# Talking-heads attention ahead of two feed-forward layers on one core: the mixed matrix and v kept in fp32 for their product, and the steps laid anew

## The chip, the cores and the metric

The kernel runs on one core of one Trainium2 chip. The metric is the device time of one execution in microseconds, the median over several runs. One further execution is recorded by the hardware profiler; every row below is from it.

## What is computed

```python
# q, k, v: (4, 12, 448, 64); w_pre, w_post: (12, 12)
scores = np.matmul(q, k.transpose(0, 1, 3, 2)) / 8
scores = np.einsum('bhij,hg->bgij', scores, w_pre)      # mix the heads
scores = scores - np.max(scores, axis=-1, keepdims=True)
attn = np.exp(scores)
attn = attn / (np.sum(attn, axis=-1, keepdims=True) + 1e-09)
attn = np.einsum('bhij,hg->bgij', attn, w_post)         # mix the heads again
x = np.matmul(attn, v)                                  # -> (1792, 768)
h = x @ w_in;  x = (h * np.cos(h)) @ w_out              # 768 -> 2048 -> 768
g = x @ w_gate                                          # 768 -> 1536
out = (g / (1 + np.exp(-g)) * (x @ w_val)) @ w_out2     # 1536 -> 768
```

All inputs and the output are fp32.

## The kernel before

**Attention.** Each of the 4 batches is cut along the queries into 4 chunks, and a chunk into 12, 12, 11 or 10 blocks (`CH`) of 10 queries by 12 heads. So there are 45 blocks in a batch and 180 in all. A block passes through these functions, one after another:

- `premix` (line 220): TensorE multiplies the block's scores, 120 rows by 448 keys, by a block matrix of w_pre. Both are fp32; each such matmul stands in the trace as two matmul records.
- `rowmax` (225, VectorE), `expo` (233, ScalarE), `den` (240) and `rec` (244, VectorE): the softmax.
- `norm_hi` (249, GpSimd) and `norm_lo` (256, VectorE): the normalized block as an fp16 value and an fp16 rest.
- `post` (269 to 271): 12 fp16 matmuls by w_post, 3 for each quarter of the keys. The result lies transposed in PSUM, 112 keys by 480.
- `at_hi` (282, ScalarE) and `at_lo` (290, VectorE): that result, copied out as fp16 value and fp16 rest.

Once for each chunk and pair of heads `m` (six of them) come two more products:

- `qk` (195): scores of the next chunk, 6 matmuls, 3 for each head of the pair; the two heads use different rows of TensorE. `spread` (211, 213) copies each head's scores to SBUF and sends them by a DMA on SP's queue into `x`, laid out for `premix`. `qk` uses the two PSUM banks `ps_s`.
- `pv` (302): the mixed matrix times v. v is split by `split_v` (176, 179, 182) into fp16 value and rest, so there are 12 products for each head: 4 quarters of the keys by 3 terms. The two heads use different columns of TensorE and lie in turn in the program. Three `m` share one of the two banks `ps_v`. `pv_out` (319, 320) takes three `m` out of PSUM.

v is loaded twice. The first time (`vm`) it is only read for its largest value (`max_v`, 148), from which `scale_v` makes a power of two, by way of a small TensorE matmul (`pow2_b`, 83). The second time (`vr`) it is scaled and split.

The order is written out by hand. `plan` holds for each step `i` which functions run; block `i` does `premix` at step `i` and each later function a fixed lag behind. `QK_STEPS` and `PV_STEPS` say at which steps of a chunk the six `qk` and `pv` stand. Inside a step, `order` sets the order of the functions, and so the order of the instructions on each engine. `dma_k`, `dma_q` and `dma_v` stand in the plan in the same way; all of these DMAs are issued on SP's queue.

**Feed-forward.** During the last chunk `early_plan` begins with the first layer (`l1_part`, 732 to 734; `hidden`, 749 to 762). After the attention `FeedForward.steps` runs the rest: weights are loaded, scaled and split (567 to 606), and `l2` (777 to 783) adds to the result. The change leaves this code as it is.

Of the kernel before, what the change touches and what calls it, by code (L numbers as in the profile page):

```python
# [20 lines left out]
DM = H * D  # L21
# [19 lines left out]
def attention(ctx, tc, qT, kT, vN, mix, xs, ff):  # L41
# [39 lines left out]
    def pow2_b(diag, n, name):  # L81
        ps = ps_v.tile([128, 512], F32, tag="pv", name=f"psp_{name}")
        nc.tensor.matmul(ps[:, :n], ones[:n, :], diag[:n, :n], start=True, stop=True)
        return ps
# [13 lines left out]

    ff.ps_sum = lambda name: ps_v.tile([128, 512], F32, tag="pv", name=name)
    ktiles, qtiles, vtiles, vscale = {}, {}, {}, {}  # L100
# [36 lines left out]

    def dma_v(b, jc, why):
        r = p_vr.tile([112, DM], F32, tag="vr", name=f"v{why}_{b}_{jc}")
        nc.sync.dma_start(r, vN[b, :, jc])  # L140
        raws["v", why, b, jc] = r

    vmx = {}

    def max_v(b, jc):
        if jc == 0:
            vmx[b] = p_small.tile([112, 4], F32, tag="vmx", bufs=2, name=f"vmx_{b}")
        nc.vector.tensor_reduce(
            out=vmx[b][:, jc:jc + 1], in_=raws.pop(("v", "m", b, jc)), axis=AX.X, op=ALU.max,
            apply_absolute_value=True,  # L150
        )
# [3 lines left out]
    def scale_v(b, part):  # L155
        if part == 1:
            scales[b] = pow2_b(scales[b], 112, f"v{b}")
            return
        if part == 2:
            p = pow2_c(scales[b], 112, f"v{b}")  # L160
            nc.vector.tensor_scalar(
                ff.unit[0][:, b:b + 1], p[:, 0:1], pw[:, 0:1], 2.0 ** -9, op0=ALU.mult, op1=ALU.mult
            )
            vscale[b] = p
            return
        m1 = p_small.tile([112, 1], F32, tag="vmx1", bufs=2, name=f"vmx1_{b}")
        nc.vector.tensor_reduce(out=m1, in_=vmx[b], axis=AX.X, op=ALU.max)
        scales[b] = pow2_a(m1, 112, f"v{b}")

    def split_v(b, jc, part):  # L170

        r = raws["v", "r", b, jc]
        rv = r.rearrange("p (m e d) -> p m e d", e=2, d=D)
        by = vscale[b][:112, 1:2]
        if part == 0:
            nc.scalar.activation(r, r, AF.Copy, scale=by)
        elif part == 1:
            t = vtiles[b, jc] = p_v.tile([112, 6, 2, 2, D], F16, tag="v", name=f"v_{b}_{jc}")
            nc.vector.tensor_copy(t[:, :, :, 0], rv)
        else:  # L180
            t, m = vtiles[b, jc], slice(3 * part - 6, 3 * part - 3)
            nc.gpsimd.tensor_tensor(t[:, m, :, 1], rv[:, m], t[:, m, :, 0], op=ALU.subtract)

    X, SP, SMALL, PM, E, EHL, PA, AT, PV = ({} for _ in range(9))

    def qk(b, c, m, places=((ps_s, "s"),)):

        n = 10 * CH[c]
        for e in range(2):
            pool, tag = places[(2 * m + e) % len(places)]  # L190
            SP[b, c, 2 * m + e] = pool.tile([128, 512], F32, tag=tag, name=f"pss_{b}_{c}_{2 * m + e}")
        for i, (zq, zk) in enumerate(((0, 0), (1, 0), (0, 1))):
# [80 lines left out]

    def at_hi(b, c, k):
        n = CH[c]
        if k == 0:
            AT[b, c] = tuple(
                p_at.tile([112, n, 4 * H, 10], F16, tag=f"at{z}", padded_shape=[112, 12, 4 * H, 10],
                          name=f"at{z}_{b}_{c}")
                for z in range(2)  # L280
            )
        nc.scalar.activation(
            AT[b, c][0][:, k].rearrange("p g i -> p (g i)"), PA[b, c, k][:112, :480], AF.Copy,
            scale=2.0 ** -4,
        )

    def at_lo(b, c, k):
        src = PA.pop((b, c, k))[:112, :480]
        th, tl = (t[:, k].rearrange("p g i -> p (g i)") for t in AT[b, c])
        nc.vector.scalar_tensor_tensor(tl, src, 2.0 ** -4, th, op0=ALU.mult, op1=ALU.subtract)  # L290

    def pv(b, c, m):


        n = 10 * CH[c]
        if m % 3 == 0:
            PV[b, c, m // 3] = ps_v.tile([128, 4, 128], F32, tag="pv", name=f"psv_{b}_{c}_{m}")
        ps = PV[b, c, m // 3]
        prods = [(jc, zv, za) for jc in range(4) for zv, za in ((0, 0), (0, 1), (1, 0))]
        for i, (jc, zv, za) in enumerate(prods):  # L300
            for e in range(2):
                nc.tensor.matmul(  # L302
                    ps[64 * e:64 * e + 64, m % 3, :n].rearrange("p (k i) -> p k i", i=10),
                    vtiles[b, jc][:, m, e, zv], AT[b, c][za][:, :, jc * H + 2 * m + e],
                    start=(i == 0), stop=(i == len(prods) - 1),
                )

    def pv_out(b, c, g3):
# [10 lines left out]
        nc.scalar.activation(hi, ps[:, :, :r], AF.Copy, scale=2.0 ** -5)  # L319
        nc.vector.scalar_tensor_tensor(lo, ps[:, :, :r], 2.0 ** -5, hi, op0=ALU.mult, op1=ALU.subtract)  # L320
        if not direct:
# [13 lines left out]
    for i, blk in enumerate(blocks):  # L335
        for fn, lag in ((premix, 0), (rowmax, 1), (expo, 1), (den, 2), (rec, 3), (norm_hi, 3),
                        (norm_lo, 4), (post, 6), (at_hi, 7), (at_lo, 7)):
            at(i + lag, fn, *blk)
    for ci, (b, c) in enumerate(chunks):
        n, s0 = CH[c], first[b, c]  # L340
        if ci + 1 < len(chunks):
            nb, ncn = chunks[ci + 1]
            for m in range(6):
                i = s0 + QK_STEPS[n][m]
                at(i, qk, nb, ncn, m)
                for e in range(2):
                    at(i + 1, spread, nb, ncn, 2 * m + e)
            if ci:
                at(s0 - 7, dma_q, nb, ncn)
                for e in range(2):  # L350
                    at(s0 - 2 + e, hi_q, nb, ncn, e)
                    at(s0 - 1 + e, lo_q, nb, ncn, e)
        if c == 2 and b + 1 < B:
            for m in range(6):
                i = s0 + 1 + 14 * m // 6
                at(i - 1, dma_k, b + 1, m)
                at(i + 2, hi_k, b + 1, m)
                at(i + 3, lo_k, b + 1, m)
        if c == 0:
            if b == 0:  # L360
                for part in range(3):
                    at(4 + part, scale_v, 0, part)
            if b + 1 < B:
                for part in range(3):
                    at(first[b, 3] + 7 + part, scale_v, b + 1, part)
            for jc in range(4):
                if b == 0:
# [7 lines left out]
                if b + 1 < B:  # L375
# [10 lines left out]
    for i, fn, *a in ff.early_plan(first[B - 1, 3]):  # L386
        at(i, fn, *a)

    order = (
        "rec", "pv_out", "pv", "post", "at_hi", "l1_part", "rowmax", "dma_v", "at_lo", "w_sum",  # L390
        "w_sum_all", "w_unit", "w_bits", "hidden", "den", "max_v", "scale_v", "hi_k", "dma_q",
        "lo_q", "spread", "split_v", "dma_k", "w_dma", "x_load", "load_next", "new_scale", "hi_q",
        "w_max", "w_shift", "w_split", "expo", "norm_hi", "premix", "qk", "lo_k", "norm_lo",
    )


    with tc.manual_schedule():
# [580 lines left out]
```

## Time and profile before

| | |
|---|---|
| median of 3 runs | 1462.12 us (1461.84 to 1464.26) |
| the profiled execution: its time, its span | 1462.24 us, 1460.4 us |
| span, PE busy | 1408.3 us, 96% |
| span, DVE / ACT / POOL busy | 73% / 44% / 34% |
| the first block's `premix`, the last chunk's first `premix` | 22.1 us, 435.0 us |
| matmuls of the feed-forward alone from | about 493 us |

PE is TensorE, PEld its weight loads, DVE VectorE, ACT ScalarE, POOL GpSimd, SP the queue that issues most DMAs. Matmuls are pipelined: a matmul's recorded time is longer than its share of the stream. So the time that a group of matmuls takes is read from its first start to the first start of the next group.

### The profile page before, as it was taken

What the parts mean: (1) busy time and instruction counts of PE and PEld (TensorE: products, weight loads), DVE (VectorE), ACT (ScalarE), POOL (GpSimd) and SP (SyncE); (2) the same over time, 40 slices, a digit from 0 to 9 for tenths busy, and PEclk for the clock granted to TensorE, in tenths of its full rate; (3) what the DMA queues carried; (4) which work ended last, traced back from release to release, by engine and by line L of the source; (5) the groups of instructions that cost most, each with busy time, mean ns of one, the idle gap of its engine ahead of it and who ended that gap; (6) DMA issues with size and microseconds to landing.
All of it is one profiled execution on the core that took longest, in us unless ns stands there. A gap on an engine that the chain in (4) does not pass through costs nothing.

```text
span 1460.4 us, 27063 instructions
## 1 busy us (share of the span) xinstructions
PE 1408.3 (96%) x10330; PEld 940.7 (64%) x10330; DVE 1068.1 (73%) x2310; ACT 646.3 (44%) x1374; POOL 494.4 (34%) x522
## 2 busy tenths in 40 slices
PE   6999999999999899999999999989999999999999
PEld 2556666656665566767676766656666666666666
DVE  5888989888988667878888878786355656565523
ACT  3777877877865353333333332444422223222210
POOL 2553553553532233323333332332223223222210
PEclk9999999999999999999999999999999999999999
DMA  6555555555546112121212221021112212211013
GB/s 203 147 155 152 154 157 157 149 156 149 156 140 226 44 55 77 54 66 54 77 54 66 65 65 44 22 65 55 55 44 66 66 44 69 62 55 33 1 38 114
DMA packets 102264, 131.77 MB, mean 90 GB/s; under 512 B 29848, under 2 KB 88696, under 8 KB 102136
## 3 DMA queue, kind: packets, MB, share of 16 engines
q1 hardware_dynamic: 101296, 128.77, 29.8%
q8 instruction: 81, 1.33, 0.4%
q10 hardware_dynamic: 840, 1.29, 0.3%
q14 instruction: 47, 0.39, 0.1%
HBM read 80.95 MB, written 10.37 MB: 63 GB/s over the span
## 4 chain that ended last, share of the span: by engine, by line
PE 76%; DVE 15%; ACT 4%; DMA 3%; issue 2%; SPq 0%; POOL 0%; ACTq 0%; DVEq 0%; POOLq 0%
PE ph L732 10%; PE ph L734 10%; PE ph L733 10%; PE psm L220 9%; PE py L777 7%; PE py L778 7%; PE py L779 7%; PE pss L195 5%; PE psv L302 4%; PE psa L269 3%; PE psa L270 2%; PE psa L271 2%; DVE acc L783 2%; DVE r L750 2%; DVE r L753 2%
## 5 line engine op out<-in xcount | busy, mean ns | idle before, releaser
L732 PE MATMUL ph<-x,h_i 128*128 128x448 f16 x960 | 339.4, 354 | 0.0
L733 PE MATMUL ph<-x,h_i 128*128 128x448 f16 x960 | 338.9, 353 | 0.0
L734 PE MATMUL ph<-x,l_i 128*128 128x448 f16 x960 | 338.9, 353 | 0.0
L762 POOL TENSOR_TENSOR gl<-r,gh 128x448 fp32r<-128x448 f32 x112 | 131.6, 1175 | 411.4 <-ACT gh L761 406.1
L777 PE MATMUL py<-gh,h_o 128*128 128x448 f32 x672 | 257.8, 384 | 11.5 <-DVE acc L783 6.2
L778 PE MATMUL py<-gl,h_o 128*128 128x448 f32 x672 | 245.5, 365 | 0.0
L779 PE MATMUL py<-gh,l_o 128*128 128x448 f32 x672 | 245.2, 365 | 0.1
L783 DVE TENSOR_TENSOR acc<-py,acc 128x448 f32<-128x448 f32 x288 | 174.4, 619 | 64.2 <-PE py L779 60.3
L220 PE MATMUL psm<-x,wpre_sb 120*120 120x448 f32 x360 | 181.1, 586 | 17.8 <-DMA x<-s 7.1
L249 POOL TENSOR_SCALAR eh<-e,sm 120x448 f16<-120x448 f32 x180 | 115.0, 639 | 183.8 <-DVE sm L244 113.9
L732 PEld LDWEIGHTS <-h_i 128*128 128x128 f16 x960 | 93.9, 98 | 92.4 <-issue 10.6
L777 PEld LDWEIGHTS py<-gh,h_o 128*128 128x128 f32 x672 | 127.3, 189 | 37.1 <-DVE acc L783 16.9
L734 PEld LDWEIGHTS <-l_i 128*128 128x128 f16 x960 | 94.0, 98 | 87.9 <-issue 0.4
L733 PEld LDWEIGHTS <-h_i 128*128 128x128 f16 x960 | 94.2, 98 | 82.0 <-issue 0.2
L225 DVE TENSOR_REDUCE sm<-psm 120x1 f32<-120x448 f32 x180 | 110.6, 615 | 41.7 <-PE psm L220 40.2
L233 ACT ACTIVATE e<-psm,sm 120x448 f32<-120x448 f32 x180 | 115.7, 643 | 56.9 <-DVE sm L225 55.1
L606 POOL TENSOR_TENSOR l_i<-f_i,h_i 128x384 f16<-128x384 f32 x80 | 81.3, 1016 | 174.9 <-ACT h_i L605 174.7
L760 DVE SCALAR_TENSOR_TENSOR r<-ph,by_i,r 128x448 f32<-128x448 f32 x48 | 32.8, 684 | 146.5 <-PE ph L734 115.8
L269 PE MATMUL psa<-wpost,eh 120*112 120x120 f16 x720 | 131.8, 226 | 4.9 <-DVE at L290 2.3
L779 PEld LDWEIGHTS py<-gh,l_o 128*128 128x128 f32 x672 | 127.0, 189 | 10.3 <-POOL l_o L606 1.3
L778 PEld LDWEIGHTS py<-gl,h_o 128*128 128x128 f32 x672 | 127.4, 190 | 7.5
L761 ACT CAST gh<-r 128x448 fp32r<-128x448 f32 x112 | 63.5, 567 | 155.0 <-DVE r L760 117.8
(105 smaller groups left out, 2451.3 us busy)
## 6 DMA issues: line engine op xcount, KB each, us to landing
r_o<-in_w_out SPq DMA_DIRECT2D x56, 384.0 KB
x<-s SPq DMA_DIRECT2D x84, 210.0 KB
r_i<-in_w_in SPq DMA_DIRECT2D x32, 384.0 KB
x<-s SPq DMA_DIRECT2D x48, 192.5 KB
r_i<-in_w_gate SPq DMA_DIRECT2D x24, 384.0 KB
r_i<-in_w_val SPq DMA_DIRECT2D x24, 384.0 KB
x<-s SPq DMA_DIRECT2D x48, 175.0 KB
qr<-in_qT SPq DMA_DIRECT2D x15, 360.0 KB
```

The source lines that it names most:

```text
L220: nc.tensor.matmul(ps[:120, :S], wpre_sb, X[b, c][:120, k], start=True, stop=True)
L233: nc.scalar.activation(e, PM.pop((b, c, k))[:120, :S], AF.Exp, bias=sm[:, 0:1], scale=1.0, accum_out=sm[:, 1:2])
L249: nc.gpsimd.tensor_scalar(eh, E[b, c, k], sm[:, 3:4], 1.0, op0=ALU.mult, op1=ALU.mult)
L269: nc.tensor.matmul(o, eh[:, j], wpost_sb[0], start=True, stop=False)
L732: nc.tensor.matmul(ps, wh, xh, start=(kk == 0), stop=False)
L733: nc.tensor.matmul(ps, wh, xl, start=False, stop=False)
L734: nc.tensor.matmul(ps, wl, xh, start=False, stop=(kk == 5))
L762: nc.gpsimd.tensor_tensor(gl, r, f(gh), op=ALU.subtract)
L777: nc.tensor.matmul(ps, wh, gh[:, e], start=(e == 0), stop=False)
L778: nc.tensor.matmul(ps, wh, gl[:, e], start=False, stop=False)
L779: nc.tensor.matmul(ps, wl, gh[:, e], start=False, stop=(e == 1))
L783: nc.vector.tensor_tensor(acc, ps, acc, op=ALU.add)
```

## The change

The mixed matrix is copied out of PSUM once, as fp32 (`mixed_out`, by ScalarE, and by VectorE for three blocks of a chunk), in place of `at_hi` and `at_lo`. v stays as it was loaded, in fp32; `split_v` and the second load are gone. `pv` has 4 fp32 products for each head in place of 12 fp16 ones. The scale of v is now applied in `pv_out`.

`qk`, `pv` and the small matmuls of `pow2_b` draw their banks from one ring of four (`bank`). `QK_STEPS` and `PV_STEPS` now put two `qk`, and three or six `pv`, into one step. A new order (`ORDER`) and new lags move most functions; q is loaded and split earlier, and v's largest value is taken later.

```diff
-QK_STEPS = {12: (0, 1, 3, 5, 7, 8), 11: (0, 4, 5, 6, 7, 8), 10: (0, 2, 3, 5, 6, 7)}
-PV_STEPS = {11: (13, 13, 13, 15, 17, 17), 12: (11, 11, 11, 13, 15, 17), 10: (10, 10, 10, 14, 16, 16)}
+LAGS = (0, 1, 1, 2, 2, 3, 4, 6, 7)
+QK_STEPS = {12: (2, 2, 6, 6, 8, 8), 11: (2, 2, 4, 4, 6, 8), 10: (0, 0, 4, 4, 6, 6)}
+PV_STEPS = {12: (10, 10, 10, 10, 10, 10), 11: (10, 10, 10, 13, 13, 13), 10: (8, 8, 8, 11, 11, 11)}
+SECOND = 1
+Q_STEPS = (-10, -6, -3)
+K_STEPS = (1, 3, 5, 8, 10, 12)
+V_STEPS = (4, 8, 12, 16)
+AT_DVE = (2, 5, 8)
+ORDER = (
+    "scale_v", "mixed_out", "l1_part", "norm_hi", "dma_v", "spread", "post", "rowmax", "w_sum",
+    "w_sum_all", "w_unit", "w_bits", "hidden", "norm_lo", "den", "w_max", "w_shift", "w_split",
+    "expo", "lo_q", "dma_q", "lo_k", "qk", "rec", "premix", "pv_out", "hi_k", "dma_k", "w_dma",
+    "x_load", "load_next", "new_scale", "max_v", "pv", "hi_q",
+)
-    p_s = pool("a_s", 5, SB, scores, "right")
+    p_s = pool("a_s", 6, SB, scores, "right")
-    p_vr = pool("a_vr", 3, SB, scores, "right")
+    def bank(name):
+
+        second = len(banks) % 4 > 1 or "closed" in banks
+        banks.append(name)
+        pool, tag = (ps_v, "pv") if second else (ps_s, "s")
+        return pool.tile([128, 512], F32, tag=tag, name=name)
...
-    def split_v(b, jc, part):
...
-    def at_hi(b, c, k):
+    def mixed_out(b, c, k):
...
+        if k in AT_DVE:
+            nc.vector.tensor_scalar(to, src, 2.0 ** -15, None, op0=ALU.mult)
+        else:
+            nc.scalar.activation(to, src, AF.Copy, scale=2.0 ** -15)
...
-        prods = [(jc, zv, za) for jc in range(4) for zv, za in ((0, 0), (0, 1), (1, 0))]
-        for i, (jc, zv, za) in enumerate(prods):
+        for jc in range(4):
             for e in range(2):
                 nc.tensor.matmul(
                     ps[64 * e:64 * e + 64, m % 3, :n].rearrange("p (k i) -> p k i", i=10),
-                    vtiles[b, jc][:, m, e, zv], AT[b, c][za][:, :, jc * H + 2 * m + e],
-                    start=(i == 0), stop=(i == len(prods) - 1),
+                    vtiles[b, jc][:, m, e], AT[b, c][:, :, jc * H + 2 * m + e],
+                    start=(jc == 0), stop=(jc == 3),
                 )
...
             for jc in range(4):
-                if b == 0:
-                    if jc == 3:
-                        at(1, dma_v, 0, jc, "m")
-                    at(jc, max_v, 0, jc)
-                v0 = s0 + 4 * jc + 5
-                at(v0, dma_v, b, jc, "r")
-                for part in range(4):
-                    at(v0 + 2 + part, split_v, b, jc, part)
-                if b + 1 < B:
-                    i = first[b, 3]
-                    at(i + jc, dma_v, b + 1, jc, "m")
-                    at(i + jc + 2, max_v, b + 1, jc)
+                v0 = s0 + V_STEPS[jc]
+                at(v0, dma_v, b, jc)
+                at(v0 + 4, max_v, b, jc)
+            for part in range(3):
+                at(v0 + 5 + part, scale_v, b, part)
...
-    order = (
-        "rec", "pv_out", "pv", "post", "at_hi", "l1_part", "rowmax", "dma_v", "at_lo", "w_sum",
-        "w_sum_all", "w_unit", "w_bits", "hidden", "den", "max_v", "scale_v", "hi_k", "dma_q",
-        "lo_q", "spread", "split_v", "dma_k", "w_dma", "x_load", "load_next", "new_scale", "hi_q",
-        "w_max", "w_shift", "w_split", "expo", "norm_hi", "premix", "qk", "lo_k", "norm_lo",
-    )
...
-        for jc in range(3):
-            dma_v(0, jc, "m")
```

## Rows read from the trace of the kernel before

**Rows 1.** The page's first part: busy time, share of the span, instructions.
```profile
PE 1408.3 (96%) x10330; PEld 940.7 (64%) x10330; DVE 1068.1 (73%) x2310; ACT 646.3 (44%) x1374; POOL 494.4 (34%) x522
```

**Rows 2.** Windows: us; busy (x instructions) of PE, PEld, DVE, ACT, POOL; PEclk; DMA share; GB/s.
```profile
22.00:53.30 31.30, 26.65 (x146) 13.80 (x147) 21.53 (x61) 18.12 (x43) 11.89 (x15) 0.89 0.65 185
...
106.10:215.00 108.90, 106.85 (x1353) 69.39 (x1354) 97.70 (x257) 82.99 (x201) 54.53 (x67) 0.98 0.53 154
...
435.00:500.00 65.00, 55.99 (x722) 37.96 (x723) 50.85 (x117) 30.26 (x66) 18.86 (x22) 0.88 0.51 161
```

**Rows 3.** Timeline of PE, undisturbed stretches: start, length, line, tiles, shapes, count.
```profile
85.83 0.97 PE L220 MATMUL psm<-x,wpre_sb 120*120 120x448 f32 x2
86.64 0.22 PE L269 MATMUL psa<-wpost,eh 120*112 120x120 f16 x1
...
87.27 0.97 PE L220 MATMUL psm<-x,wpre_sb 120*120 120x448 f32 x2
88.17 0.85 PE L195 MATMUL pss<-k,q 64*100 64x448 f32 x6
88.95 0.83 PE L302 MATMUL psv<-at,v 112*64 112x120 f16 x24
...
219.58 2.10 PE L302 MATMUL psv<-at,v 112*64 112x120 f16 x72
221.61 0.26 PE L269 MATMUL psa<-wpost,eh 120*112 120x120 f16 x1
```

**Rows 4.** Groups by line and form: count, busy us, mean ns of one.
```profile
L290 DVE SCALAR_TENSOR_TENSOR at<-psa,at 112x480 f16<-112x480 f32 x180 | 116.8, 649 | 6.6 <-ACT at L282 6.4 <-DMA x<-s 0.2
L282 ACT ACTIVATE at<-psa 112x480 f16<-112x480 f32 x180 | 103.1, 573 | 2.1 <-PE psa L271 1.8
L749 DVE TENSOR_SCALAR k<-ph,by_i 128x448 int32<-128x448 f32 x64 | 43.6, 681 | 42.2 <-PE ph L734 34.4 <-PE su_i L547 5.9
```

**Rows 5.** Timeline of PE: the small fp32 matmul, the premix behind it.
```profile
347.55 0.43 PE L83 MATMUL psp_v<-diag_v,ones 112*128 112x112 f32 x2
347.82 0.92 PE L220 MATMUL psm<-x,wpre_sb 120*120 120x448 f32 x2
```

**Rows 6.** Groups by line: weight loads of PE.
```profile
L302 PEld LDWEIGHTS <-v 112*64 112x64 f16 x2304 | 60.7, 109 | 31.3 <-issue 31.3
L220 PEld LDWEIGHTS psm<-x,wpre_sb 120*120 120x120 f32 x360 | 53.8, 190 | 21.7 <-issue 10.7 <-ACT at L282 5.7 <-ACT e L233 2.7
```

**Rows 7.** Timeline of PE around a late premix: the first and last of four.
```profile
102.15 0.23 PE L269 MATMUL psa<-wpost,eh 120*112 120x120 f16 x1
...
106.07 1.48 PE L220 MATMUL psm<-x,wpre_sb 120*120 120x448 f32 x2 [3.12 <-DMA x<-s]
107.48 1.47 PE L195 MATMUL pss<-k,q 64*120 64x448 f32 x6
...
431.40 0.23 PE L269 MATMUL psa<-wpost,eh 120*112 120x120 f16 x1
...
435.03 1.82 PE L220 MATMUL psm<-x,wpre_sb 120*120 120x448 f32 x2 [2.82 <-issue]
```

**Rows 8.** Timeline of SP's queue before the first of them.
```profile
97.47 3.96 SPq L213 DMA_DIRECT2D x<-s  x4
...
102.03 0.41 SPq L140 DMA_DIRECT2D vm<-in_vN  x1
```

**Rows 9.** The chain that ended last, in the first chunk: start, length, what.
```profile
26.11 6.71 DMA vm<-in_vN
...
46.15 4.78 DMA vr<-in_vN
```

**Rows 10.** Timeline of PE where attention ends and the second product begins.
```profile
486.56 1.75 PE L302 MATMUL psv<-at,v 112*64 112x100 f16 x70 [1.50 <-DVE at L290]
490.76 2.06 PE L302 MATMUL psv<-at,v 112*64 112x100 f16 x72 [2.46 <-DVE x L320]
493.24 0.74 PE L777 MATMUL py<-gh,h_o 128*128 128x448 f32 x1 [0.42 <-ACT h_o L605]
```

More of the change, by code (lines that the diff above doesn't have):

```diff
@@ L67, in attention @@
     ps_m = pool("ps_m", 2, PSUM, mixed)
+    banks = []
+    def bank(name):
[3 more added lines that the diff above has]
+        return pool.tile([128, 512], F32, tag=tag, name=name)
     ones = const.tile([128, 128], F32, name="ones")
@@ L81, in pow2_b @@
     def pow2_b(diag, n, name):
-        ps = ps_v.tile([128, 512], F32, tag="pv", name=f"psp_{name}")
+        ps = bank(f"psp_{name}")
         nc.tensor.matmul(ps[:, :n], ones[:n, :], diag[:n, :n], start=True, stop=True)
@@ L97, in pow2_c @@
         return p
-    ff.ps_sum = lambda name: ps_v.tile([128, 512], F32, tag="pv", name=name)
+    ff.ps_sum = bank
     ktiles, qtiles, vtiles, vscale = {}, {}, {}, {}
@@ L136, in lo_q, with dma_v @@
         eng.tensor_tensor(lo, raws["q", b, c][:, 3 * e:3 * e + 3], f(hi), op=ALU.subtract)
[L138 to L141, printed above, removed]
+    def dma_v(b, jc):
+        t = vtiles[b, jc] = p_v.tile([112, 6, 2, D], F32, tag="v", name=f"v_{b}_{jc}")
+        nc.sync.dma_start(t.rearrange("p m e d -> p (m e d)"), vN[b, :, jc])
     vmx = {}
@@ L148, in max_v @@
         nc.vector.tensor_reduce(
-            out=vmx[b][:, jc:jc + 1], in_=raws.pop(("v", "m", b, jc)), axis=AX.X, op=ALU.max,
+            out=vmx[b][:, jc:jc + 1], in_=vtiles[b, jc].rearrange("p m e d -> p (m e d)"), axis=AX.X, op=ALU.max,
             apply_absolute_value=True,
@@ L163, in scale_v @@
             )
-            vscale[b] = p
+            vscale[b] = const.tile([128, 1], F32, tag="xo_scale", bufs=2, name=f"xo_scale_{b}")
+            nc.vector.tensor_scalar(vscale[b], p[:, 1:2], 64.0, None, op0=ALU.mult)
             return
@@ L168, in scale_v, with qk @@
         scales[b] = pow2_a(m1, 112, f"v{b}")
-    def split_v(b, jc, part):
[L172 to L182, printed above, removed]
     X, SP, SMALL, PM, E, EHL, PA, AT, PV = ({} for _ in range(9))
-    def qk(b, c, m, places=((ps_s, "s"),)):
+    def qk(b, c, m, places=()):
         n = 10 * CH[c]
         for e in range(2):
-            pool, tag = places[(2 * m + e) % len(places)]
-            SP[b, c, 2 * m + e] = pool.tile([128, 512], F32, tag=tag, name=f"pss_{b}_{c}_{2 * m + e}")
+            name = f"pss_{b}_{c}_{2 * m + e}"
+            if places:
+                pool, tag = places[(2 * m + e) % len(places)]
+                SP[b, c, 2 * m + e] = pool.tile([128, 512], F32, tag=tag, name=name)
+            else:
+                SP[b, c, 2 * m + e] = bank(name)
         for i, (zq, zk) in enumerate(((0, 0), (1, 0), (0, 1))):
@@ L272, in post @@
         PA[b, c, k] = ps
-    def at_hi(b, c, k):
+    def mixed_out(b, c, k):
         n = CH[c]
         if k == 0:
[L277 to L280, printed above, removed]
-            )
[L282 to L290, printed above, removed]
+            AT[b, c] = p_at.tile([112, n, 4 * H, 10], F32, tag="at", padded_shape=[112, 12, 4 * H, 10],
+                                 name=f"at_{b}_{c}")
+        to, src = AT[b, c][:, k].rearrange("p g i -> p (g i)"), PA.pop((b, c, k))[:112, :480]
+        if k in AT_DVE:
+            nc.vector.tensor_scalar(to, src, 2.0 ** -15, None, op0=ALU.mult)
+        else:
+            nc.scalar.activation(to, src, AF.Copy, scale=2.0 ** -15)
     def pv(b, c, m):
@@ L318, in pv_out @@
             hi, lo = x[:, 0, :, :r], x[:, 1, :, :r]
-        nc.scalar.activation(hi, ps[:, :, :r], AF.Copy, scale=2.0 ** -5)
-        nc.vector.scalar_tensor_tensor(lo, ps[:, :, :r], 2.0 ** -5, hi, op0=ALU.mult, op1=ALU.subtract)
+        by = vscale[b]
+        nc.scalar.activation(hi, ps[:, :, :r], AF.Copy, scale=by)
+        nc.vector.scalar_tensor_tensor(lo, ps[:, :, :r], by, hi, op0=ALU.mult, op1=ALU.subtract)
         if not direct:
@@ L335, in attention @@
     for i, blk in enumerate(blocks):
-        for fn, lag in ((premix, 0), (rowmax, 1), (expo, 1), (den, 2), (rec, 3), (norm_hi, 3),
-                        (norm_lo, 4), (post, 6), (at_hi, 7), (at_lo, 7)):
+        for fn, lag in zip(
+            (premix, rowmax, expo, den, rec, norm_hi, norm_lo, post, mixed_out), LAGS
+        ):
             at(i + lag, fn, *blk)
@@ L345, in attention @@
                 at(i, qk, nb, ncn, m)
+                late = m and QK_STEPS[n][m - 1] == QK_STEPS[n][m]
                 for e in range(2):
-                    at(i + 1, spread, nb, ncn, 2 * m + e)
+                    at(i + (SECOND if late else 1), spread, nb, ncn, 2 * m + e)
             if ci:
-                at(s0 - 7, dma_q, nb, ncn)
+                at(s0 + Q_STEPS[0], dma_q, nb, ncn)
                 for e in range(2):
-                    at(s0 - 2 + e, hi_q, nb, ncn, e)
-                    at(s0 - 1 + e, lo_q, nb, ncn, e)
+                    at(s0 + Q_STEPS[1] + e, hi_q, nb, ncn, e)
+                    at(s0 + Q_STEPS[2] + e, lo_q, nb, ncn, e)
         if c == 2 and b + 1 < B:
             for m in range(6):
-                i = s0 + 1 + 14 * m // 6
+                i = s0 + K_STEPS[m]
                 at(i - 1, dma_k, b + 1, m)
@@ L440, in attention @@
                 scores.close()
+                banks.append("closed")
                 ff.open_early()
@@ L444, in attention @@
                 ff.open_ps()
-            for kind in order:
+            for kind in ORDER:
                 for fn, a in plan.pop((i, kind), []):
```

9 lines of the change are left out of this document (1 added, 8 removed).

## The prediction, made before the changed kernel was run

> **What bounds the kernel now.** I read the page first. PE is busy 96% of the span, VectorE 73% [rows 1]. A busy PE proves little, since matmuls overlap in the pipeline, so next come the windows by stage [rows 2]. All that the change touches ends near 500 us; the feed-forward behind it keeps its code, and I take its 960 us as they are. In the attention one batch takes 108.9 us, with PE busy 106.9, VectorE 97.7, ScalarE 83.0 and GpSimd 54.5. Two engines are nearly full. Which of them sets the pace is read from PE's timeline [rows 3], start to start. `premix` takes 0.81 us (85.83 to 86.64) and `post` 0.63. Ahead of a `qk` a `premix` holds 0.90 instead, a `qk` 0.78, and three `m` of `pv` 2.03. So entering a product that uses part of the rows or columns costs about 0.10.
>
> The batch from these prices: 45 `premix` x 0.80 = 36.0; 45 `post` x 0.65 (0.63 to 0.67) = 29.2; 24 `qk` x 0.88 = 21.1. `post` streams 120 columns in 0.63 / 12 = 0.0525, and `pv` does a pair of heads in the same time: 2.03 is 36 x 0.053 and 0.12 to drain. The two heads run side by side. Over a batch (two chunks of 120 columns, one of 110, one of 100) that is 14.3 us, 14 visits x 0.12 = 1.7, and 0.7 for entries: 16.7. Together 103.0 us of 108.9. PE is the bound; VectorE's load matters only by some 6 us of stalls in a batch.
>
> Where these stalls lie: the first `premix` of the fourth chunk comes late in every batch [rows 7]. From `post` to that `premix` 3.92 us pass in place of 0.65, and the `premix` behind it holds 1.41 in place of 0.90: PE is at half its clock after the idle time. I price the first at 4.8 us, with the `qk` and `post` that still run slowly, the last at 5.8, and the two between at about 4: 19 us for four. The queue shows why [rows 8]: four sends of `x` in a row end at 101.4, the last data land at 106, and the first load of `vm` follows them.
>
> **The change, part by part.**
>
> *Other engines.* VectorE loses 45 `at_lo` of 0.649 in a batch and gains 12 `mixed_out`, priced by the nearest row, a scalar product out of PSUM of 0.681 [rows 4]: 97.7 - 29.2 + 8.2 = 76.7. ScalarE gives 12 of 45 copies of 0.573 away: 83.0 - 6.9 = 76, and less without the scaling of v. GpSimd loses v's split. None of them nears 104, so a copy or a reduction that moves costs nothing while PE's work covers it; were the cover gone, VectorE's 77 would still not bind.
>
> *`pv` in fp32.* No row shows an fp32 product with two heads on different columns. A single fp32 product is shown twice: 448 columns in 0.81, so 1.80 ns a column; and 112 columns in 0.27, so 2.4 ns, where the product is short and its loads show [rows 3, 5]. If two heads still run side by side, a quarter of the keys costs a pair 120 x 1.80 = 0.216, and by four times the fp16 pair 0.21. A batch has 24 such pairs in each of four chunks, 450 columns in all: 24 x 450 x 1.75 to 1.80 ns = 18.9 to 19.4, and 6 visits x 0.22: 20.5 against 16.7. That is +3.8, or +15 for four batches. By the short product it is 25.9 + 1.3: +10.5, or +42. One after another at 1.80 it is 38.9 + 1.3: +23.5, or +94. I take +15: the fp16 pairs show side by side, and a stream of products hides loads as the long product does.
>
> A weight load with 64 fp16 columns takes 0.109, with 120 fp32 columns 0.190 [rows 6], so an fp32 load of 64 lies between; half a product streams for 0.10. In the fp16 stream such loads cost nothing: a pair takes 0.053, less than one load. The Trainium skill (TensorE: Matmul & The Clock Gate, Part 3, The mechanism) says that weight loads overlap running matmuls only where the row group differs, and the two heads of `pv` share their rows. By that rule loads would stand in the stream, and the time would be that of the second rival below in its part form; the fp16 rows speak against it.
>
> *Merged `qk`.* A visit of one `qk` costs 0.88: 0.10 to enter, three pairs of 0.20 (a quarter of a `premix`), 0.18 to drain. A second one in the visit saves 0.28. In the steady plan 90 visits become 49 (4 x 10 + 9): 41 x 0.28 = -11.5. Bounds: 0 if each `qk` still drains, -15.
>
> *The late fourth chunk.* Its last `qk` stays at step 8, but four of the sends move two steps ahead, `vm` is gone from the queue, and three `m` of `pv` (2.5 us) now stand at step 10, between that `qk` and the late `premix`. The wait of 3.1 us should be gone and the clock stay up: -16 of 19; bounds -4 to -19, with the small stalls -23.
>
> *The start.* On the chain of waits the first chunk has a landing of `vm` of 6.71 and one of `vr` of 4.78 [rows 9]. VectorE and ScalarE wait for them, and what is queued behind (the `rowmax`, the `expo`) holds up `premix`. `max_v` now stands four steps behind its load, and `scale_v` at step 21. That chunk takes 31.3 us at a granted clock of 0.89, a steady one 27.2 [rows 2]. The sends of `x` on the same queue remain: -5; bounds 0 and -11.5.
>
> *The end.* PE waits 1.50 for the last `at_lo` and 2.46 for a `pv_out`, and the 65 us show a clock of 0.88 and 9 us idle [rows 2, 10]. `norm_hi` now stands ahead of `hidden` on GpSimd, and all six `m` of the last chunk go at one step: -8; bounds 0 and -13.
>
> *What the new plan adds.* Two `qk` need all four banks of the ring, so PE waits for four copies, or for a `pv_out`, before it; queued behind are `premix` and with it `rowmax`. Four copies also stand ahead of an `expo`: about 2.3 us at the price of the PSUM copy [rows 4]. PE covers that with two `premix` and a `post` (2.25). The cover is barely enough: I put +4, bounds 0 and +15. The other moves of q, k and the small matmul of `scale_v` lie steps ahead of their use, and I cost them at nothing; PE's stream hides them.
>
> Sum: 15 - 11.5 - 16 - 5 - 8 + 4 = -21.5. The profiled execution took 1462.24 (its span 1460.4 and 1.8 around it), within 0.2 us of the median, so the forecast is 1441 us, its own range 1425 to 1456.
>
> **The rivals.**
>
> 1. *The gain is larger*: all small stalls go as well (-23), start and end reach -9 and -12, and the plan adds nothing. 15 - 11.5 - 23 - 9 - 12 = -40: 1422. For it speaks that every engine but PE gets slack; against it that sends of `x` are as many as before.
>
> 2. *The two heads of an fp32 pair don't run side by side* (slower). Place: the stream of `pv`. In full it gives 94 in place of 15: 1441 + 79 = 1520. In part, a pair waits for one load of 64 columns, 0.109 [rows 6], and costs 0.21 + 0.11 = 0.32, 1.5 times my price; that is 19.2 x 0.5 = 9.6 more in a batch: 1441 + 39 = 1480. It decides from the point where `pv` eats the other gains, 36.5 us over four batches: 16.7 + 9.1 - 1.3 = 24.5 us / (24 x 450) = 2.27 ns a column, a pair of 120 columns at 0.27. For it: the short fp32 product shows 2.4 ns. Against it: that product stands alone, and heads overlap in every row of `qk` and `pv`.
>
> 3. *The stalls only move*: `x` lands as late as before because the last `qk` stands where it stood, and the bursts of four copies cost what the rest gives. 15 - 11.5 - 4 - 2 - 3 + 4 = -1.5: about 1460.
>
> **How the numbers follow.** Forecast 0.56, first rival 0.12, third 0.12, second 0.20 (half of it in full, half in part). The predicted time is the forecast's, 1441. For 8 in 10 the range leaves out the second rival and little else: 1418, just below the first, to 1468, past the third with its bursts at their bound. A change below 0.2%, 3 us, can't be told from none. Faster: 0.56 + 0.12 + half of the third = 0.74. The same: 0.06. Slower: 0.20.
>
> **What would show it.** A visit of six `m` with 120 columns should take about 5.3 us; 7.8 would be the second rival in part, 10.5 in full. A visit of two `qk` should hold 1.4. Starts of `premix` from batch to batch should be about 104 to 105 apart, VectorE busy for some 77 of them, and the fourth chunk's first `premix` without a wait for `x`. The first chunk, which ends at 53.3 [rows 2], should end near 48. If `premix` waits for a bank or `expo` behind four copies, the third rival holds. The forecast is wrong if a pair costs over 0.27, or if a new wait of a microsecond turns up in every chunk.

## The result and the profile after

After the change the kernel takes 1437.01 us (1436.59 to 1437.15, 4 runs) against 1461.98 (1461.32 to 1464.26, 4 runs): a ratio of 0.9826, 95% interval 0.9809 to 0.9843. The forecast was 1441, its range 1418 to 1468. The profiled execution took 1436.59, with a span of 1434.8 against 1460.4.

The first view is the page's first part, then the windows of the stretches shown before.

```profile
PE 1391.5 (97%) x9562; PEld 962.2 (67%) x9562; DVE 1016.1 (71%) x2166; ACT 615.2 (43%) x1310; POOL 458.8 (32%) x490
```

```profile
22.30:50.30 28.00, 21.10 (x145) 12.86 (x145) 18.55 (x49) 15.98 (x41) 10.24 (x14) 0.95 0.69 203
50.30:105.70 55.40, 54.73 (x552) 38.72 (x552) 44.45 (x116) 39.02 (x97) 25.38 (x31) 0.96 0.46 135
105.70:210.00 104.30, 104.05 (x1162) 75.81 (x1161) 84.85 (x221) 74.86 (x185) 47.11 (x59) 1.00 0.51 147
...
418.20:474.00 55.80, 49.55 (x530) 34.98 (x528) 47.30 (x105) 28.24 (x60) 19.52 (x23) 0.97 0.61 198
```

The page says little: PE's share goes from 96% to 97%. The windows say where the time went. A batch takes 104.30 in place of 108.90 [rows 2], PE is busy for all of it but 0.25, and its granted clock is 1.00. Set against the starts of the `premix` of the fourth chunks (106.07 and 435.03 before, 105.73 and 418.17 after) and of the feed-forward's `l2` (493.24, and 467.53 after), the 25.55 us of span divide so:

| stretch | before | after | difference |
|---|---|---|---|
| start to the fourth chunk of the first batch | 106.07 | 105.73 | -0.35 |
| from there to the fourth chunk of the last batch | 328.95 | 312.44 | -16.51 |
| from there to `l2` | 58.21 | 49.36 | -8.85 |
| feed-forward | 967.11 | 967.27 | +0.16 |

The timeline of PE after, undisturbed stretches, from start to start as in [rows 3]:

```profile
72.72 5.14 PE L304 MATMUL psv<-at,v 112*64 112x120 f32 x96
77.80 0.26 PE L279 MATMUL psa<-wpost,eh 120*112 120x120 f16 x1
...
117.24 0.97 PE L230 MATMUL psm<-x,wpre_sb 120*120 120x448 f32 x2
...
118.76 1.48 PE L205 MATMUL pss<-k,q 64*120 64x448 f32 x12
120.17 1.01 PE L230 MATMUL psm<-x,wpre_sb 120*120 120x448 f32 x2
...
129.94 0.97 PE L230 MATMUL psm<-x,wpre_sb 120*120 120x448 f32 x2
130.84 2.48 PE L304 MATMUL psv<-at,v 112*64 112x110 f32 x48
133.25 0.26 PE L279 MATMUL psa<-wpost,eh 120*112 120x120 f16 x1
```

Six `m` of `pv` with 120 columns take 5.08 (5.3 forecast), three with 110 columns 2.41, and a visit of two `qk` holds 1.41 (1.4 forecast). By the single records the two heads of a pair start 6 ns apart, and the next two follow after 0.094. The groups by line show the loads and the copies:

```profile
L304 PE MATMUL psv<-at,v 112*64 112x120 f32 (+2 forms) x1536 | 79.2, 260 | 0.0
L293 ACT ACTIVATE at<-psa 112x480 f32<-112x480 f32 x132 | 75.2, 569 | 3.3 <-PE psa L281 3.3
L304 PEld LDWEIGHTS psv<-at,v 112*64 112x64 f32 x1536 | 74.0, 136 | 14.9 <-issue 14.9
...
L291 DVE TENSOR_SCALAR at<-psa 112x480 f32<-112x480 f32 x48 | 30.8, 642 | 0.0
```

An fp32 load of 64 columns takes 136 ns, between the two of [rows 6], and each of 1536 matmul records has one. PE's waits (those over 0.15 us) between 105.7 and 330 us come to 1.2 us in all:

```profile
PE psm L230 <- ACT e L243: 0.8, 2, 0.6
PE pss L205 <- ACT s L221: 0.4, 1, 0.4
```

### The profile page after: what moved, and what is told of

It is laid out like the page before. It is cut to its first block, busy times and chain, and to the rows that moved or that the text cites. A ratio compares the mean times of both kernels' runs of the same rounds, so it can differ in the third digit from the quotient of the medians.

```text
span 1434.8 us, 25102 instructions
## 1 busy us (share of the span) xinstructions
PE 1391.5 (97%) x9562; PEld 962.2 (67%) x9562; DVE 1016.1 (71%) x2166; ACT 615.2 (43%) x1310; POOL 458.8 (32%) x490
## 4 chain that ended last, share of the span: by engine, by line
PE 77%; DVE 15%; ACT 3%; DMA 2%; issue 1%; SPq 0%; POOL 0%; ACTq 0%; DVEq 0%; POOLq 0%
PE ph L715 10%; PE ph L717 10%; PE ph L716 10%; PE psm L230 9%; PE py L760 7%; PE py L761 7%; PE py L762 7%; PE psv L304 5%; PE pss L205 4%; PE psa L279 2%; PE psa L280 2%; PE psa L281 2%; DVE acc L766 2%; DVE r L733 2%; DVE r L736 2%; DVE k L732 2%
## 5 line engine op out<-in xcount | busy, mean ns | idle before, releaser
L259 POOL TENSOR_SCALAR eh<-e,sm 120x448 f16<-120x448 f32 x180 | 120.9, 672 | 248.6 <-DVE sm L254 164.3
L230 PE MATMUL psm<-x,wpre_sb 120*120 120x448 f32 x360 | 179.0, 581 | 12.7 <-DMA v<-in_vN 5.5
L266 DVE SCALAR_TENSOR_TENSOR el<-e,sm,eh 120x448 f16<-120x448 f32 x180 | 135.4, 752 | 0.0
```

The lines of the kernel that those rows point to most:

```text
L230: nc.tensor.matmul(ps[:120, :S], wpre_sb, X[b, c][:120, k], start=True, stop=True)
L259: nc.gpsimd.tensor_scalar(eh, E[b, c, k], sm[:, 3:4], 1.0, op0=ALU.mult, op1=ALU.mult)
L266: nc.vector.scalar_tensor_tensor(el, E.pop((b, c, k)), sm[:, 3:4], eh, op0=ALU.mult, op1=ALU.subtract)
```

## The experiments

All were timed beside the kernel before on the same chip (1460.35, 1460.86 and 1460.82 us in the three groups of runs: `e1` to `e4`; `e5`, `e6`, `e7`, `e9`; the last four). The change itself was timed in another group (1461.98 for the kernel before), so a difference to it is uncertain by 1 to 2 us.

### Does a pair of heads run side by side in fp32?

`e1_heads_in_turn`: the loops of `pv` change places, so that the four products of one head stand ahead of those of the other.

```diff
-        for jc in range(4):
-            for e in range(2):
+        for e in range(2):
+            for jc in range(4):
```

> The changed kernel, but each m of pv does the four products of one head and then the four of the other, in place of the two heads in turn. Theory (the pair of heads runs side by side, and that is why a pair of 120 columns costs 0.21 us): now two half-products of the same head follow each other, and the heads meet only where one ends and the other begins, one half-product in eight; an m of 120 columns goes from 0.83 to about 1.5, 96 m cost some 65 us more: about 1500 us (1485 to 1515). Rival (fp32 products are that cheap by themselves, or TensorE pairs them whatever the order): 1437, within 3.

1454.88 us (1453.36 to 1455.52), ratio 0.9962 [0.9947, 0.9978]: 18 more than the change, where the theory had 63 and the rival none. The timeline of PE, the visit that takes 2.41 after:

```profile
133.79 3.14 PE L304 MATMUL psv<-at,v 112*64 112x110 f32 x48
136.86 0.26 PE L279 MATMUL psa<-wpost,eh 120*112 120x120 f16 x1
```

3.07 for 48 matmul records. The single records show why it isn't twice 2.41. They form six rows of eight, one for each head of the three `m`, and inside a row they start 0.146 and from then on 0.094 apart. Each row begins 0.434 behind the one before it, just after that one's fifth record, so the last three of one head lie between the first three of the next. The records don't name the head; this is read from their spacing. So the theory's mechanism holds, its size doesn't: by this reading products on other columns go ahead of products that stand before them in the program.

`e9_all_columns`: each product is given the v of both heads, 128 columns, into all rows of the bank. This leaves out that the heads are kept apart. Products and loads are as many as before, but no two can lie side by side.

```diff
-    ps[64 * e:64 * e + 64, m % 3, :n]...  vtiles[b, jc][:, m, e], ...  start=(jc == 0), stop=(jc == 3)
+    ps[:, m % 3, :n]...  vtiles[b, jc][:, m] (both e), ...  start=(jc == 0 and e == 0), stop=(jc == 3 and e == 1)
```

> The changed kernel with each product of pv given both heads' v as weights, 128 columns, so that no two products can run side by side; the two heads' products are added up, so this leaves out keeping the heads apart, and its output is not the attention's. Theory (a pair of heads costs 0.21 us in fp32 because two products share TensorE by columns): an m of 120 columns goes from 0.83 to about 1.65, 96 m cost some 76 us more: about 1512 us (1495 to 1525). Rival (the pairing gives little for fp32): under 1460.

1525.06 us (1523.82 to 1526.62), ratio 1.0438 [1.0419, 1.0458]: the theory's case. The timeline of PE, again 110 columns:

```profile
134.99 0.97 PE L230 MATMUL psm<-x,wpre_sb 120*120 120x448 f32 x2
135.79 5.51 PE L304 MATMUL psv<-at,v 112*128 112x110 f32 x48
141.13 0.22 PE L279 MATMUL psa<-wpost,eh 120*112 120x120 f16 x1
```

5.34 in place of 2.41, and 88 us in all. That is the second rival in full, and somewhat more: the loads of 128 columns take 192 ns in place of 136, and the records start 0.11 apart in place of 0.094, by which 48 of them would take 4.5. This experiment, `e1` and the starts 6 ns apart show that a pair runs side by side.

### The two halves of the change, each alone

`e2_old_plan_fp32`: the kernel before with its plan, order and banks, but v loaded raw, one fp32 copy and the fp32 product.

```diff
-        prods = [(jc, zv, za) for jc in range(4) for zv, za in ((0, 0), (0, 1), (1, 0))]
+        for jc in range(4):
...
+        if k in AT_DVE:
+            nc.vector.tensor_scalar(to, src, 2.0 ** -15, None, op0=ALU.mult)
```

> The kernel before with the arithmetic alone changed: mixed matrix copied out once as fp32, pv in four fp32 products, v not split; the old steps, order and banks, and the separate first load of v for its maximum. Theory (TensorE sets the pace, the gain is in the plan): pv costs 19 us more over 96 m, no visit is saved, the four late first premix of the fourth chunk mostly stay; less work on VectorE gives back some 4 us of small stalls and some 6 at the start and the end: about 1470 us (1462 to 1476). Rival (the gain comes from what VectorE, ScalarE and GpSimd no longer do): 1450 or less.

1468.41 us (1465.94 to 1470.85), ratio 1.0054 [1.0033, 1.0074], as the theory has it. VectorE's load falls and gives nothing, since in the old plan it isn't what PE waits for: PE's longest waits here are for `vm` (3.2), at an issue (2.8) and for `x` (2.5). All three stand ahead of a fourth chunk's first `premix`.

`e3_new_plan_fp16`: the changed kernel with the fp16 split put back (`at_hi`, `at_lo`, `split_v`, 12 products for each head).

```diff
-                for jc in range(4): ... vtiles[b, jc][:, m, e], AT[b, c]
+        for i, (jc, zv, za) in enumerate(prods): ... vtiles[b, jc][:, m, e, zv], AT[b, c][za]
...
+        nc.vector.scalar_tensor_tensor(tl, src, 2.0 ** -4, th, op0=ALU.mult, op1=ALU.subtract)
```

> The new plan with the old arithmetic: steps, order, ring of banks and single load of v as changed, but at and v split into fp16 value and rest, 12 products for a head (v is split unscaled, its scale stays behind the product; one staging buffer of s less, three for v). Theory (both: TensorE bound with VectorE close behind): pv gives 19 us back, and VectorE, with the second half of the copies and 98 us of work in a batch of 100, becomes a second bound: some 2 to 4 us of stalls in a batch; 1437 - 19 + 8 to 16: about 1430 us (1424 to 1438), so fp32 gains little or loses a little by itself. Rival A (TensorE alone): 1418. Rival B (VectorE binds without the fp32 product): over 1445.

1467.59 us (1465.62 to 1469.56), ratio 1.0041 [1.0026, 1.0057]. The theory had 1430; the rival is right. So each half alone makes the kernel slower by 0.4 to 0.5%, and both together make it faster by 1.7%. A batch, and PE's longest wait in 60 to 430 us, of this kernel (windows and waits):

```profile
112.20:223.20 111.00, 103.81 (x1354) 70.30 (x1353) 102.76 (x258) 80.13 (x198) 62.79 (x67) 1.00 0.48 139
PE psa L289 <- DVE at L310: 19.9, 28, 1.2
```

VectorE is busy for 102.76 of 111.00, and PE waits 28 times for `at_lo` to give back one of the two banks that `post` writes. Two things could do that: VectorE's load, or the place of `at_lo` in the step. The next three runs ask which, and answer it in part.

`e8_all_on_vector` and `e11_all_on_scalar`: the changed kernel with all, or none, of its copies `mixed_out` on VectorE.

```diff
-AT_DVE = (2, 5, 8)
+AT_DVE = tuple(range(12))     # e8_all_on_vector
+AT_DVE = ()                   # e11_all_on_scalar
```

> All twelve columns of a chunk's mixed_out go to VectorE (twelve where the change has three). A batch moves 33 copies of 0.64 us there, 21 us, to VectorE's 85 busy us, and takes about 19 from ScalarE. Theory (VectorE, not ScalarE, was what let the new plan fail with the fp16 split): with 85 + 19 to 21 = 104 to 106 VectorE stands level with PE's 104.3, its stalls come back in every batch, the batches take 107 to 111 and the time is 1447 to 1465. Rival (bursts of copies matter, VectorE's load does not): no more than 1441.

1461.68 us (1458.53 to 1465.01), ratio 1.0002 [0.9988, 1.0015]: the theory's case. Windows and waits of this kernel:

```profile
105.60:216.70 111.10, 106.99 (x1161) 76.39 (x1160) 103.57 (x254) 59.33 (x153) 43.39 (x59) 1.00 0.48 139
PE psm L230 <- ACT e L243: 7.8, 16, 0.6
```

VectorE's load is that of `e3` (103.57 of 111.10) and so is the batch, with no `at_lo` at all. ScalarE has 15.5 us less to do than in the change, and yet PE waits for `expo`, which stands behind `rowmax` on VectorE. For the bank of `post` PE waits 1.6 us in all (60 to 430 us), so the bank isn't the cause here. With VectorE at about 104 us in a batch 24.7 us go, nearly all that the change brings. Not parted from the load is the copy's place: it stands ahead of `rowmax` in its step and makes `rowmax` and `expo` later too.

> The other end of the same term: no mixed_out on VectorE, twelve of a chunk on ScalarE. A batch takes 12 copies, 7.7 us, from VectorE's 85 and gives ScalarE 12 x 0.57 = 6.8 to its 75. Theory (VectorE's 85 leaves slack enough, PE sets the pace): 1437, within 3 us. Rival (the bursts of four copies ahead of an expo are what the split over two engines avoids, the +4 of the forecast): 1441 to 1447.

1433.55 us (1432.6 to 1433.73), ratio 0.9806 [0.9789, 0.9824]: 0.4 below the theory's range, and the rival's bursts of copies cost nothing. Its median is the lowest of this study, 3.5 below the change. That it is faster than the change isn't shown: they were not timed in one group, and the intervals of the two ratios overlap. A batch of it (windows), in which no wait of PE is listed:

```profile
104.40:208.40 104.00, 103.96 (x1162) 75.72 (x1160) 78.97 (x209) 80.78 (x198) 47.52 (x59) 1.00 0.52 149
```

`e12_fp16_lo_last`: `e3` with `at_lo` last in its step.

```diff
-    ... "post", "rowmax", "at_lo", "w_sum", ...  "max_v", "pv", "hi_q",
+    ... "post", "rowmax", "w_sum", ...  "max_v", "pv", "hi_q", "at_lo",
```

> The new plan with the fp16 split again, with one thing changed: the VectorE copy that makes the lower half (at_lo) stands last in its step, behind rowmax, den and all else. The same work on every engine. Theory (VectorE's load, 101.5 busy us of a batch's 110, is what costs the time): 1463 to 1472 as with the other order. Rival (it was the copy's place ahead of den and the reciprocal): below 1452.

1515.89 us (1515.63 to 1517.47), ratio 1.0373 [1.0354, 1.0392]. Both missed: the place matters, and the other way round. Windows and waits:

```profile
122.00:245.90 123.90, 106.20 (x1355) 70.77 (x1353) 107.30 (x258) 82.49 (x199) 49.97 (x67) 0.99 0.44 125
PE psa L289 <- DVE at L310: 40.9, 64, 1.7
```

Here VectorE is not full (107.30 of 123.90). A late `at_lo` holds the bank, `post` waits for it, and the next `at_hi` and `at_lo` come later still. So `e3` may have both faults in some share: its 45 copies of 0.647, 29 us a batch, load VectorE, and they hold `post`'s bank. `e8` has the same load and the same 111 with hardly a wait for that bank; how the 111 of `e3` divides stays open.

### The merged `qk`

`e4_one_qk`: one `qk` to a step, 90 visits again, the last one of each chunk where it was.

```diff
-QK_STEPS = {12: (2, 2, 6, 6, 8, 8), 11: (2, 2, 4, 4, 6, 8), 10: (0, 0, 4, 4, 6, 6)}
+QK_STEPS = {12: (1, 2, 4, 6, 7, 8), 11: (1, 2, 3, 4, 6, 8), 10: (0, 1, 3, 4, 5, 6)}
```

> The changed kernel with the six qk of a chunk at six steps of their own, 90 visits in the steady plan in place of 49; the last one stays at its step. Theory (each visit that uses part of TensorE's rows costs 0.26 to 0.28 to enter and drain): 41 x 0.27 = 11 us more, 1448 us (1444 to 1452). Rival (the drain is covered, or bursts of four copies cost as much as the visits save): 1437 or less.

1449.69 us (1448.43 to 1452.4), ratio 0.9928 [0.9909, 0.9947]. Batches of 108.6 and 108.8. The change is 12.7 us faster, where the forecast had 11.5 for the merging. In a batch it is 4.3 (108.6 less 104.3) for 11 visits fewer, 0.39 each.

### The late fourth chunk

`e6_old_vm_late`: the kernel before, `vm` loaded three steps later, behind the last sends of `x` on SP's queue.

```diff
-                    at(i + jc, dma_v, b + 1, jc, "m")
+                    at(i + jc + 3, dma_v, b + 1, jc, "m")
```

> The kernel before with the first load of the next batch's v, and its maximum, three steps later (two for the scale), so that it is no longer issued behind the last sends of x for the fourth chunk. Theory (the late first premix of the fourth chunk comes from late sends and from v that shares the DMA engines with them, about half each): three of the four waits shrink by some 2 us: about 1456 us (1453 to 1459 where the kernel before gives 1461). Rival A (v is the cause): 1449 or less. Rival B (the sends alone, v has no part): 1461, within 1.5.

1465.17 us (1463.05 to 1471.62), ratio 1.0038 [1.0022, 1.0054]. The theory (1456) falls: moving the load of v gives nothing, and the time is 4 longer, which no run explains.

`e7_pv_behind`: the changed kernel, no `pv` between the last `qk` and the late `premix`.

```diff
-PV_STEPS = {..., 11: (10, 10, 10, 13, 13, 13), ...}
+PV_STEPS = {..., 11: (13, 13, 13, 14, 14, 14), ...}
```

> The changed kernel with the pv of a batch's second chunk moved from steps 10 and 13 of the third chunk to 13 and 14, behind the first premix of the fourth chunk, which it no longer covers. Theory (that premix is in time because 2.6 us of pv stand before it): it waits again for x, 1 to 2 us and a slow clock behind it, in four batches: about 1445 us (1441 to 1450). Rival (earlier sends and the missing second load of v were enough): 1437, within 2.

1438.01 us (1435.55 to 1439.16), ratio 0.9840 [0.9820, 0.9859]: the theory (1445) falls. The median is 1.0 above the change, so the cover of 2.5 us is worth little; the traces below show that it isn't worth nothing.

`e10_old_qk_early`: the kernel before, the first five sends of the fourth chunk earlier.

```diff
-QK_STEPS = {..., 11: (0, 4, 5, 6, 7, 8), ...}
+QK_STEPS = {..., 11: (0, 1, 2, 4, 6, 8), ...}
```

> The kernel before, with only the six qk of the fourth chunk issued at steps 0, 1, 2, 4, 6, 8 of the third (0, 4, 5, 6, 7, 8 before), so that their sends of x lie apart on the queue; the last one stays where it was. Theory (the late fourth chunk came from the sends in a row, as the forecast's -16 has it): its first premix waits for x a microsecond or less, and the time is 1445 to 1453. Rival (the last qk, its copy and its send alone take the time; what helped was the plan as a whole): 1458 to 1463.

1459.21 us (1452.4 to 1464.75), ratio 0.9985 [0.9967, 1.0003]: the theory falls again, and its rival is right. So neither of the causes that the prediction named, the sends in a row and `vm`, is the one. The timelines of PE from the last `qk` to the late `premix` of the same batch show another (the rows of `post` are left out); first the kernel before:

```profile
208.19 0.85 PE L195 MATMUL pss<-k,q 64*100 64x448 f32 x6
209.64 0.97 PE L220 MATMUL psm<-x,wpre_sb 120*120 120x448 f32 x2
211.07 0.97 PE L220 MATMUL psm<-x,wpre_sb 120*120 120x448 f32 x2
214.74 0.98 PE L220 MATMUL psm<-x,wpre_sb 120*120 120x448 f32 x2 [1.93 <-ACT at L282]
```

the changed kernel without the cover, `e7_pv_behind`, and the late `premix` of its last batch:

```profile
203.02 0.85 PE L205 MATMUL pss<-k,q 64*100 64x448 f32 x6
203.80 1.01 PE L230 MATMUL psm<-x,wpre_sb 120*120 120x448 f32 x2
205.28 0.97 PE L230 MATMUL psm<-x,wpre_sb 120*120 120x448 f32 x2
206.71 0.97 PE L230 MATMUL psm<-x,wpre_sb 120*120 120x448 f32 x2
208.24 1.48 PE L205 MATMUL pss<-k,q 64*120 64x448 f32 x12
210.16 0.98 PE L230 MATMUL psm<-x,wpre_sb 120*120 120x448 f32 x2 [0.44 <-ACT e L243]
...
419.87 0.98 PE L230 MATMUL psm<-x,wpre_sb 120*120 120x448 f32 x2 [1.93 <-ACT e L243]
```

and `e10_old_qk_early`:

```profile
205.26 0.84 PE L195 MATMUL pss<-k,q 64*100 64x448 f32 x6
206.71 0.97 PE L220 MATMUL psm<-x,wpre_sb 120*120 120x448 f32 x2
208.37 0.97 PE L220 MATMUL psm<-x,wpre_sb 120*120 120x448 f32 x2
212.65 1.82 PE L220 MATMUL psm<-x,wpre_sb 120*120 120x448 f32 x2 [2.04 <-ACT at L282]
```

From the start of the last `qk` to the `premix` that needs its scores 6.55 us pass before and 7.39 in `e10`, both with a wait. Both rows name a copy `at` on ScalarE, which is done just ahead of the `premix`. The rows by line show that it isn't what was late in `e10`:

```profile
L220 PEldq EVENT_SEMAPHORE  x3: 51/51/2517, 209.9 to 212.5; - x3
```

PE's sequencer stood for 2.52 us at a wait ahead of the weight load of this `premix`, and by the single records came out of it at 212.49, while the copy ended at 212.58. A transfer marks a semaphore as it lands, and the last mark of the last send of `x` is at 212.45. What is late is `x`. The same records, for the fourth chunk of all four batches, in us:

| kernel | last `qk` to the landing of its `x` | PE at work until the late `premix` | PE idle until then | landing to `premix` |
|---|---|---|---|---|
| before | 6.3 to 7.7 | 4.6 | 1.9 to 3.1 | 0.1 to 0.5 |
| `e6`, v later | 6.8 to 7.1 | 4.6 | 2.3 to 3.0 | 0.1 to 0.5 |
| `e10`, sends earlier | 6.6 to 7.2 | 4.6 to 4.8 | 1.8 to 2.6 | 0.1 to 0.4 |
| `e7`, change without cover | 6.7 to 7.0 | 6.7; last batch 5.3 | 0.04 to 0.8; last batch 1.9 | 0.1 to 0.5 |
| the change | 5.8 to 7.0 | 9.4 to 9.9; last batch 7.9 | 0 or 0.4 | 2.1 to 3.4 |

So `x` needs some 6 to 8 us from the last `qk`, whether the other sends go earlier or v later, and the `premix` starts 0.1 to 0.5 behind the landing wherever PE has less work than that. What the change brings is work in that stretch: from 4.6 to 6.7 by the order inside the step, to 9.4 with the `pv` visit. The new `ORDER` puts `qk` ahead of `premix` in its step. So the last `qk`, still at step 8, has three `premix` and `post` behind it in place of two, and the two `qk` of step 0 of the next chunk (1.41) stand ahead of the late `premix` in place of behind it. The last batch of `e7`, where no such `qk` follow, has 5.3 of work and waits 1.9 again. In its other three batches `x` lands just in time; the `pv` visit adds the margin. The old plan with only this order turned round was not run.

### The start

`e5_v_late_start`: the changed kernel, the first batch's v loaded from step 16 on.

```diff
-                at(v0, dma_v, b, jc)
+                at(v0 if b else 16, dma_v, b, jc)
```

> The changed kernel with the first batch's four loads of v moved from steps 4, 8, 12 and 16 to step 16, behind the sends of x for the second and the first of the third chunk (max_v at steps 18 to 20). Theory (the second chunk's first premix at 50.3 us waits because three loads of v, 1 MB, move on the same DMA engines as the last sends of its x): that premix comes about 5 us earlier and the slow clock behind it goes, 1432 us (1429 to 1435). Rival (the sends of x are late by themselves, or the four maxima in a row cost VectorE what is won): 1437, within 1.5.

1438.24 us (1436.26 to 1439.08), ratio 0.9841 [0.9823, 0.9860]: the theory (1432) falls. The chain of waits of the changed kernel shows why it was worth asking:

```profile
42.76 7.48 DMA v<-in_vN
50.26 1.82 PE psm L230 x2
```

With v out of the way the last `x` of the second chunk lands 5.3 us after its send in place of 8.2, and that chunk begins at 46.99 in place of 50.26. But it takes 32.6 in place of 29.6, and the third begins at 79.6 in place of 79.9. In the second chunk VectorE now waits 2.0 us for v, the four maxima stand close together behind that, and PE waits 2.7 for `expo` and for the input of the small matmul. What was won is lost there. How much of that is the transfers and how much the maxima isn't told apart; the rival named both.

## Why the prediction was right

The sum, -21.5, came out at -25.5. Its main reading held: PE sets the pace, a pair of heads runs side by side in fp32, and merged visits and stalls that vanish pay for the longer `pv`. Not each of its terms came out:

- **`pv` in fp32, +15.** Right in mechanism and nearly in size. In a batch stand one visit of six `m` with 120 columns (5.08), one with 100 (4.27), two of three `m` with 120 (2.61) and two with 110 (2.41); with six entries of 0.1 that is 20.0 against 16.7, so +13 for four batches. A pair of 120 columns costs 0.21, as priced. The Trainium skill (TensorE: Matmul & The Clock Gate, Part 3, The mechanism) has loads overlap only where the row group differs; by that rule, as an estimate, a pair would have cost 0.35, its 0.21 and a load of 136 ns. The trace doesn't agree with it here: both heads use the same rows, and all loads are hidden.
- **The second rival** was to decide from 0.27 for a pair on; the pair took 0.21. `e9` puts its full form at 88 with loads that are longer as well, the prediction at 79.
- **Merged `qk`, -11.5.** 12.7 by `e4`. From the timelines, `premix` to `premix`: a step without a `qk` takes 1.44 [rows 3], one with a `qk` 2.35 before (97.44 to 99.79), one with two 2.93 after (117.24 to 120.17). A visit saved is worth 0.34, 13.7 for 41. The price of 0.28 leaves out that `post` holds longer behind a visit, 0.68 (99.11 to 99.79).

```profile
97.44 0.97 PE L220 MATMUL psm<-x,wpre_sb 120*120 120x448 f32 x2
...
99.79 0.97 PE L220 MATMUL psm<-x,wpre_sb 120*120 120x448 f32 x2
```

- **The late fourth chunk and the small stalls, -16.** Nearly right in size, but its reason was wrong in part. Between the fourth chunks of the first and the last batch -16.5 were measured. `pv` and `qk` are worth about -1 of that in three batches (3.3 less 11 visits of 0.34 for each), so some 15 of stalls went there, where the forecast had 12 of its 16. These are the waits for `x`, the slow stretches behind them (after the first wait, of 3.1 us, the granted clock is 0.56 from 106.1 to 110.0 us, most of it at the lower level of 1.2 GHz; in a batch of the change it is 1.00) and the small stalls, which the first rival had. The prediction names three things: "four of the sends move two steps ahead, `vm` is gone from the queue, and three `m` of `pv` (2.5 us) now stand at step 10". The first two don't shorten the way of `x` (`e10`, `e6`). The third gives a margin, but three of four batches are in time without it (`e7`). The order inside the step, which the prediction passed over, gives most.
- **The start, -5**, with the first of the late chunks (some -4 of the 16) about -9 up to its fourth chunk: -0.35 measured. This is the step that failed. The prediction says that "the sends of `x` on the same queue remain" and puts no wait for them into the sum. In the change the last `x` of the second chunk is sent at 41.95, among loads of v issued at 31.2, 38.8 and 42.8 us, and lands at 50.17; PE waits 5.5 us until then. (The chain above names the last of these loads, which lands at the same time.) So the first chunk ended at 50.3, not near 48. Behind that wait the granted clock is 0.79 from 50 to 60 us, and the second chunk takes 29.6 in place of 25.7.
- **The end, -8.** -8.85.
- **The plan's own lumps, +4.** Hardly anything of it shows: 1.2 us of waits in two batches. `e11` gives all copies to ScalarE, and in a batch of it no wait of PE is listed.
- **VectorE, 77 in a batch.** 84.85. 36 instructions fewer took 12.9 away, not 21. Their durations together do fall by 19.6 in a batch (116.5 to 96.9), but the rows of VectorE overlap, and the overlap falls by 6.7 (18.8 to 12.1). Two of them in the timeline of `e10`:

```profile
208.49 0.60 DVE L225 TENSOR_REDUCE sm<-psm 120x1 f32<-120x448 f32 x1
209.01 0.64 DVE L290 SCALAR_TENSOR_TENSOR at<-psa,at 112x480 f16<-112x480 f32 x1
```

The second starts 0.08 before the first ends. Durations that are added up overrate an engine's load.

A further fault lies in the form of the sum: its terms were added as if each stood alone. `e2`, `e3` and `e8` show that they don't. With VectorE at 103 the new plan brings nothing; without the new plan a VectorE at 80 brings nothing. The prediction had priced VectorE's load at some 6 us of stalls in a batch; in the new plan a VectorE at 103 keeps the batch at 111, 7 above the change.

So the time is right to 4 us in part by luck. The start gave some 9 less than was put down, and the lumps (4), the stalls (3), the merged visits (2) and `pv` (2) together gave some 11 more.

## What to carry to other kernels

When the busiest engine leaves only a few per cent, look at the second: here the fp32 product costs TensorE 13 us and takes the second reading of PSUM from VectorE, and that paid only together with a plan in which PE hardly waits. Where a step's functions are reordered, count for each late transfer the work that now stands between its send and its use, by instruction and not by step. In `e5` a load that was moved out of one chunk cost as much in the next.

## What the runs showed of the hardware

- In `e1`, by the spacing of the records, products on one half of the columns start ahead of products on the other half that stand before them in the program, from the fifth of eight on; 3.07 us for what takes 2.41 in turn and 5.34 in `e9`, where no two can overlap and the loads are longer. The Trainium skill (TensorE: Matmul & The Clock Gate, Part 3, The mechanism) has matmuls start and end in program order; this trace differs in the starts.
- A `premix` that is followed by a product on half the columns holds 0.90 (129.94 to 130.84), one followed by `e9`'s product on all of them 0.80 (134.99 to 135.79): so the 0.10 for entering goes with the split of the columns.
